# Reading V in its own layout in the first token mixes of a fused attention and mixer kernel, with V's copy, U's cast and the zero tile moved

One core of one Trainium2 chip. The metric is the device time of one execution in microseconds (us); lower is better. Most executions agree within 0.3%. Some executions fall in a slower state, with a lower clock; every ratio below uses runs of the fast state alone, while the medians quoted are of all runs.

## The reference

Random-feature attention for 8 batches, 8 heads, 576 tokens and head size 64, then a mixer on its output:

```python
def phi(x):
    proj = np.einsum('bhsd,md->bhsm', x, omega)
    return np.concatenate([np.cos(proj), np.sin(proj)], axis=-1) / np.sqrt(m)
kv  = einsum('bhsm,bhsd->bhmd', phi(k), v);   z = sum(phi(k), axis=2)
x   = (phi(q) @ kv) / (phi(q) @ z)            # all heads side by side: (B, 576, 512)
u   = x + (x.T @ U @ V).T                     # token mix, rank 32
out = u + np.maximum(u @ w_ch1, 0) @ w_ch2    # channel mix, 512 -> 2048 -> 512
```

`U` is 576 x 32, `V` is 32 x 576. The change is in how `V` and `U` reach the token mix.

## The kernel before

The program builds a list of operations, each for one engine, and emits them in a stored order (`ORDER`) with stored buffers (`SLOTS`); engines are in-order. PE multiplies matrices; DVE (VectorE), ACT (ScalarE) and POOL (GpSimd) do the rest. Tokens are laid out as (p, j), token = 9 p + j, so a block of 64 tokens with one j has every ninth column of `V`. GpSimd (POOL) therefore makes a packed copy `Vb` after the load:

```python
NJ = 9
o_vl = pool_dma("Vl", ..., lambda _: nc.gpsimd.dma_start(V_f, moe_V.unsqueeze(0).to_broadcast([4, R, S])), ...)
def v_cast(_):
    vf = V_f.rearrange("q (p j) -> q j p", j=NJ)
    nc.gpsimd.tensor_copy(Vb[:, 0:8, :].rearrange("q (a x) p -> q a x p", a=2),
                          vf[:, 0:8, :].rearrange("q (x a) p -> q a x p", a=2))
    for n in range(2):
        nc.gpsimd.tensor_copy(Vb[:, 8 + n, :], vf[:, 8, :])
```

Batches 0 and 1 (`TMIX`) make the mixed u already transposed, on PE: four matmuls transpose x, one adds V times the low-rank product. The moving operand of that one is `Vb`. This happens four times a batch, and once a batch for the last 64 tokens in four small pairs:

```python
def up(_):
    for i in range(4):
        nc.tensor.matmul(ups.t[:, i*P:i*P+P], x.t[:, i, cs], ident, start=(i == 0), stop=False)
    nc.tensor.matmul(ups.t, hu.t[:, cs], Vb[:, 0:8, :], start=False, stop=True)      # 128x512
def upt(_):                                                                          # tails
    for ct in range(NCT):
        ...
        nc.tensor.matmul(o, hu.t[:, c], Vb[:, 8, :], start=False, stop=(ct == NCT - 1))   # 128x64
```

Later batches use `Vb` as stationary operand. Until 36 us of planned time the program pads PE with matmuls on a tile `zero`, meant to keep its clock up; `zero` is set with other small tiles (`fills`) on DVE. U's cast to bf16 runs on POOL.

## Time and profile before

| | before |
|---|---|
| time, median (range of the 3 runs known then) | 359.13 us (358.83 to 359.60) |
| span of the profiled run | 356.7 us |
| PE busy in 28.3 to 352.3 us | 323.7 of 324.0 us |
| first w1 matmul on PE | 32.4 us |

The span is the time from the first to the last instruction in the trace; the device time is some 2 us more. Until 28 us attention of the first batch runs at the pace of DVE and ACT (the front); from there PE has work without a break until the end (the body). Anything that adds PE work in the body adds to the time one to one. The 512-column matmul that the change touches has this row (columns: busy us, mean ns of one, idle us before):

```profile
L763 PE MATMUL pb<-Vb,hu 128*128 128x512 bf16 x8 | 3.0, 379 | 0.0
L774 PE MATMUL pb<-Vb,hu 128*128 128x64 bf16 x8 | 0.7, 192 | 0.0
```

379 ns is start to modelled end. What one costs PE in a stream is the distance to the next start; the chain shows it, for the same kernel (columns: start us, us, what):

```profile
29.97 0.22 PE pb L762 x4
30.20 0.22 PE pb L763
30.41 0.22 PE pb L762 x4
30.64 0.22 PE pb L763
```

So 0.22 us for the V matmul (L763), and as much for the four transposes of x (L762). Further words used below: an eviction is a copy out of PSUM, the memory in which matmul results land; a norm is DVE's division of one head pair's result by its sum, four to a batch, each started by a RECIPROCAL; a pair is two heads; w1 and w2 are the two products of the channel mix; hu is the low-rank product x.T @ U; the tails are the last 64 tokens.

### The profile page before, as it was taken

The page shows a single profiled execution, that of the slowest core. Times are in us where ns is not written, and L with a number is a line of the kernel's source. Part 1 is how long each engine was busy: PE and PEld are TensorE (multiplying, and loading weights), DVE is VectorE, ACT ScalarE, POOL GpSimd, SP SyncE. Part 2 cuts the span into 40 slices and gives each one's busy share as a digit, 9 for nine tenths or more (in the row PEclk, how much of TensorE's full clock was granted, in tenths as well). Part 3 has the DMA queues.
Part 4 walks back from the last instruction along what each step waited for, and adds up shares of the span by engine and source line. Part 5 has one row for each costly group of instructions (what it writes and reads, how often), then busy time and mean ns, then how long its engine had stood idle before and what let it go on. Part 6 is the DMA issues. An engine that isn't in the chain of part 4 may idle for free.

```text
span 356.7 us, 9538 instructions
## 1 busy us (share of the span) xinstructions
PE 343.7 (96%) x4102; PEld 188.7 (53%) x4102; DVE 256.8 (72%) x423; ACT 210.1 (59%) x270; POOL 83.1 (23%) x148
## 2 busy tenths in 40 slices
PE   5879999999999999999999999999999999999994
PEld 3666566555557554555545554565455544555541
DVE  5999998887876787898688887886887663342221
ACT  3998998678847675557573868673676621202000
POOL 8795617511022028115041110100000000000000
PEclk9989999999999999999999999999999999999999
DMA  8999999994458999588679623891041115004114
GB/s 142 173 183 206 181 197 173 187 117 69 91 88 123 196 162 180 109 113 153 100 123 161 109 39 71 131 176 21 15 102 34 32 44 118 2 2 112 37 31 118
DMA packets 67403, 39.45 MB, mean 111 GB/s; under 512 B 47264, under 2 KB 61600, under 8 KB 67360
## 3 DMA queue, kind: packets, MB, share of 16 engines
q0 software_dynamic: 17376, 18.36, 34.6%
q1 hardware_dynamic: 49904, 20.34, 32.3%
q8 instruction: 32, 0.52, 0.6%
q10 hardware_dynamic: 80, 0.13, 0.1%
q14 instruction: 11, 0.09, 0.1%
HBM read 37.11 MB, written 9.44 MB: 130 GB/s over the span
## 4 chain that ended last, share of the span: by engine, by line
PE 90%; DVE 6%; issue 1%; ACT 1%; DMA 1%; SPq 0%
PE pb L917 34%; PE pb L863 31%; PE pp L703 5%; PE pb L882 4%; PE pp L718 4%; PE pp L618 2%; DVE cc L680 2%; PE pp L830 2%; PE pb L632 1%; DVE tt L655 1%; PE pp L724 1%; DVE tt L666 1%; PE pb L594 1%; PE pb L789 1%; DMA om_f<-in_omega_dram 1%
## 5 line engine op out<-in xcount | busy, mean ns | idle before, releaser
L863 PE MATMUL pb<-uT,W1b 128*128 128x512 bf16 x512 | 122.6, 379 | 0.0
L917 PE MATMUL pb<-W2b,hid 128*128 128x512 bf16 x512 | 122.5, 379 | 0.0
L810 ACT ACTIVATE hid<-pb 128x512 bf16<-128x512 f32 x87 | 50.6, 596 | 58.3 <-PE pb L863 58.2
L687 ACT ACTIVATE f<-cc 128x1152 bf16<-128x1152 int16 (+1 forms) x64 | 73.4, 1160 | 12.9 <-DVE cc L680 11.8
L684 ACT ACTIVATE f<-tt 128x1152 bf16<-128x1152 int16 (+1 forms) x64 | 73.6, 1160 | 7.7 <-DVE tt L655 4.8
L917 PEld LDWEIGHTS <-hid 128*128 128x128 bf16 x512 | 48.1, 98 | 55.5 <-issue 2.9
L863 PEld LDWEIGHTS <-W1b 128*128 128x128 bf16 x512 | 47.6, 98 | 55.8 <-issue 3.5
L680 DVE TENSOR_SCALAR cc<-tt 128x1152 int32<-128x1152 int16 (+1 forms) x64 | 50.2, 790 | 0.9
L582 POOL COPY v<-vraw 128x576 bf16<-128x576 bf16 x32 | 21.7, 681 | 95.5 <-PE pp L625 69.9
L808 DVE TENSOR_SCALAR hid<-pb 128x512 bf16<-128x512 f32 x41 | 27.9, 687 | 17.8 <-PE pb L863 17.7
L655 DVE CAST tt<-pp 128x1024 int32<-128x1024 f32 x32 | 38.9, 1216 | 1.6 <-PE pp L618 1.5
L664 DVE CAST tt<-pb 128x512 int32<-128x512 f32 x48 | 32.4, 685 | 8.3 <-PE pb L632 8.3
L951 DVE TENSOR_TENSOR o<-pb,x 128x512 f32<-128x512 f32 x24 | 16.5, 689 | 25.5 <-PE pb L917 25.5
L733 DVE TENSOR_TENSOR x<-pp,rc 128x640 bf16<-128x640 f32 x32 | 26.4, 825 | 1.1
L703 PEld LDWEIGHTS <-f 64*128 64x128 bf16 x1152 | 20.0, 95 | 10.7 <-issue 5.8
L553 POOL DMA_DIRECT2D qk<-in_q_dram x32 | 17.9, 563 | 31.3 <-DMA qkt<-qk 27.4
L703 PE MATMUL pp<-v,f 64*128 64x65 bf16 x1152 | 23.6, 192 | 0.9 <-ACT qkt L804 0.7
L718 PEld LDWEIGHTS <-f 128*128 128x128 bf16 x512 | 20.6, 99 | 7.3 <-issue 1.7
L718 PE MATMUL pp<-kvb,f 128*128 128x65 bf16 x512 | 21.8, 195 | 1.5 <-DVE x L733 1.3
L553 POOL DMA_DIRECT2D qk<-in_k_dram x31 | 17.1, 555 | 22.0 <-DMA qkt<-qk 17.2
L835 DVE TENSOR_TENSOR x<-pp,x 128x1024 bf16<-128x1024 f32 (+1 forms) x18 | 18.6, 1043 | 4.8 <-PE pp L830 4.4
L581 POOL DMA_DIRECT2D vraw<-in_v_dram x32 | 18.8, 588 | 6.5 <-DMA W2b<-in_moe_w_ch_dram 3.8
(81 smaller groups left out, 296.3 us busy)
## 6 DMA issues: line engine op xcount, KB each, us to landing
out_dram<-o SPq DMA_DIRECT2D x71, 128.0 KB, 2.4
qk<-in_q_dram POOLq DMA_DIRECT2D x32, 144.0 KB, 5.1
vraw<-in_v_dram POOLq DMA_DIRECT2D x32, 144.0 KB, 6.0
qk<-in_k_dram POOLq DMA_DIRECT2D x31, 144.0 KB, 5.4
W1b<-in_moe_w_ch_dram POOLq DMA_DIRECT2D x2, 1024.0 KB, 11.2
W2b<-in_moe_w_ch_dram POOLq DMA_DIRECT2D x4, 512.0 KB, 13.8
uT<-x SPq DMA_TRANSPOSE x30, 2.5
qkt<-qk SPq DMA_TRANSPOSE x24, 4.8
```

Of the source, the lines that this page charges most:

```text
L553: nc.gpsimd.dma_start(qk.t[:, lo:lo + NJ, :], src[b, 2 * hp:2 * hp + 2].rearrange("h (p j) d -> (h p) j d", j=NJ))
L655: o_kc = add("kcp", "DVE", 1.14, rank, lambda _: nc.vector.tensor_copy(i32(tt.t)[:, 1280:2304], kps.t.rearrange("p a b -> p (a b)")), deps ...
L664: nc.vector.tensor_copy(i32(tt.t)[:, 640 * lo:640 * lo + 512], t.t)
L680: nc.vector.tensor_scalar(out=i32(cc.t)[:, 0:n], in0=tt.t[:, lo:lo + n, 0], scalar1=16384.0, scalar2=None, op0=ALU.add)
L684: nc.scalar.activation(out=fe.t[:, 1, lo:hi], in_=tt.t[:, lo:hi, 0], func=ACT.Sin, scale=SIN_SCALE)
L687: nc.scalar.activation(out=fe.t[:, 0, lo:hi], in_=cc.t[:, 0:n, 0], func=ACT.Sin, scale=SIN_SCALE)
L703: nc.tensor.matmul(kvp.t[:, hh, 65 * s:65 * s + 65], fe.t[pr, s, 1152 + P * jj:1280 + P * jj], v65.t[pr, KJ[jj], :], start=(jj == 0), stop ...
L718: nc.tensor.matmul(nps.t[:, hh, 65 * i:65 * i + 65], fe.t[:, s, c0:c0 + 128], kvb.t[:, hh, s, :], start=(s == 0), stop=(s == 1))
L808: nc.vector.tensor_scalar(out=o, in0=i, scalar1=0.0, scalar2=None, op0=ALU.max)
L810: nc.scalar.activation(out=o, in_=i, func=ACT.Relu)
L863: nc.tensor.matmul(hp_.t, w1h[:, ct, fs], uT.t[:, ct, 0:512], start=(ct == 0), stop=(ct == NCT - 1))
L917: nc.tensor.matmul(d, w, W2b[c4][:, f % 4, :], start=(f == 0), stop=(f == NFT - 1))
```

## The change

The intent: no wait of the first mixes for V's copy, POOL and DVE relieved in the front by moving that copy behind the first batches, U's cast off POOL, and PE padded from the first microsecond. The core of the diff; the lines of `ORDER` and `SLOTS` are replaced throughout and cut here, as are lines at the dots:

```diff
-        last = 0.3 + next(t + o.end - o.start for o, t in zip(order, at) if o.name == "fills")
+        last = 1.2
+    V_j = V_f.rearrange("q (p j) -> q j p", j=NJ)
     def fills(_):
-        nc.vector.memset(zero, 0.0)
-        nc.gpsimd.tensor_copy(Ub, U_f[:, 0:4, :])
...
-    o_uc = add("Uc", "POOL", 0.6, -4.7, u_cast, deps=o_ul + [o_z])
+        copy(_, Ub, U_f[:, 0:4, :])
...
+    o_uc = add("Uc", ("DVE", "ACT"), (0.35, 0.5), -1.62, u_cast, deps=o_ul + [o_z])
-    o_vc = add("Vc", "POOL", 1.0, -4.65, v_cast, deps=[o_vl])
+    o_vc = add("Vc", "POOL", 2.1, -0.5, v_cast, deps=[o_vl])
-            nc.tensor.matmul(ups.t, hu.t[:, cs], Vb[:, 0:8, :], start=False, stop=True)
-        o_u = add("u", "PE", 0.45, rank, up, deps=[o_hc, o_vc, o_id], uses=[ups, hu, x])
+            nc.tensor.matmul(ups.t.rearrange("q (a x p) -> q a x p", a=2, x=4), hu.t[:, cs], V_j[:, 0:8, :].rearrange(
+                "q (x a) p -> q a x p", a=2), start=False, stop=True)
+        o_u = add("u", "PE", 0.5, rank, up, deps=[o_hc, o_vl, o_id], uses=[ups, hu, x])
-                    nc.tensor.matmul(o, hu.t[:, c], Vb[:, 8, :], start=False, stop=(ct == NCT - 1))
+                    nc.tensor.matmul(o, hu.t[:, c], V_j[:, 8, :], start=False, stop=(ct == NCT - 1))
+        if b == 2:
+            o_vc.deps.append(ldq[6])
+        nc.vector.memset(zero, 0.0)          # ahead of the emitted list (comment added here)
```

The 64 elements of one j now lie 9 elements, 18 bytes, apart, and the matmul reads them so.

More of the change, by code (lines that the diff above doesn't have):

```diff
@@ L119 @@
 ORDER = """
-16 18 45 0 7 5 46 9 17a 21 23 10 73 19 6 74 22a 25 24a 12 8 49 102 28 27 101 47 50b 32 1 26 75 51 30 53 20 3 77
-170 52b 29 35 55 31 33 79 34 198 225 36 58 169 103 54 56 57 80b 37 78a 59 81 48 62 60 84 105 107 38b 83 61 2 253
-82 86 64 197 14 65 85 39 63 274 13 108b 76 273 66b 106a 226 91 109 87 89 40 67 112 110 4 11 90 88 92 113 68 93 104
-116 254 115 111 171 69 94b 41 15 117 114 95 70a 118 96 121 71 199 97 122a 119 120 123 98a 173 124 175 42b 43 44a
-72b 99 174b 125 177 1069 176b 100b 227 178 203 255 126a 127 172 334 201 181 335 180 134 204b 128b 184 231 202a 179
@@ L125 @@
-183 185 205 1071 232a 182 257 208 1070 135 200 136a 143 186 141 258b 259 142a 189 144a 206 260a 209 207 229 187
-210 190b 1072 137 188 230b 145 138a 235 211 213 131 132 275 191 212 146b 238 192 133a 129 130b 159 153 234 233
-160b 217 155 214 277 228 236 215 154a 218b 151 237 156b 261 216 149 239 264 152a 338 354 219 220 353 241 165 256
-163 150b 262 242 336 240 372 166a 245 243 355 373 263 193 164a 221 391 265 194a 267 276 357 222b 244 246b 161 266
-157 268 392 162b 167 269 168b 158a 247 248 147 376 139 270 460 337 148a 249 140a 479 278 250a 327 271 325 195 1079
@@ L130 @@
-272 324 374 326 251 279b 280 281 1080 1081 196b 328 282 1082 497 478 252b 329 331 223 393 283a 286 287a 498 224a
-1083b 330 284 333 1073 339 1074 356 332 285a 344 345 320 321a 346 312 300 302 351 340b 343 347 341 459 301a 461
-303a 308 1075 288 313b 309b 348 349 342 395 350 1076 1077a 358 363 375 364 289a 306 362 1091 352 365 359b 307a 360
-298 366 367 299a 361 292 368 310 480 394 499 293b 369 311a 371 370 1092 377 384 1093 1094 296 381 378b 1095b 1096
-383 382 386 385 379 318 380 314 1085 319b 387 297b 388 315a 396 397a 451 390 389 450 294 449 1086 316 295a 452 517
@@ L135 @@
-398 290 317a 454 463 453 1087 455 399 1088 516 400 291a 464 1089b 584 456 1109 457 401a 465a 468 462 1110 469 471
-1111 410 472 470 1112 1084 406 411 1113b 304 407 482 305a 603 1114 402 474 1097 412 1098 1099 458 473 1100 476 322
-403 483 323a 429 1101b 488 1103 1104 475 481 487 466 1078 430a 489 518 409 477 604 491 1105 500 501 490 484b 485
-493 467 486 1106 447 1107a 492 502 448b 1115 495 494 404 405 408 417 1102 418a 509 519 496 421 507 623 422a 642
-503a 585 506 510 1108 508 514 1116 520 588 709 431 512 511 586 433 1117 622 1118 1119a 1120 504 505 441 607 434a
@@ L140 @@
-437 442b 513 432a 521 445 438a 522b 605 515 577 574 425 446a 426a 419 575 578 439 420a 576 581 523 524 729 427
-440a 580 626 428b 641 579 413 435 436b 525 526a 747 414a 589 423 594 595 593 624 443 590a 767 1121 766 598 596
-1122 535 424a 643 444a 583 527 536 415 1123 582 528 587 1124 597 416b 600 1125b 601 531 602 591 606 599 645 1127
-1128 1129 1130 532 592 1131 608 612 613 616 1139 1090 537 710 615 529 1140 1141 625 1142 835 614 554 1143 609b 617
-530 534 619 533 568 748 728 569b 618 555b 627 631 562 563a 1132 711 570 1144 634 610 730 632 544 644 635 633 712
@@ L145 @@
-571a 558 620 628a 637 636 611 545a 546 547b 638 640 559b 853 1133 1134 646 702 556 1135 731 699 749 572 557b 621
-629 700 713 639 701 1136 630 548 560 647b 750 648 1137 732 1145 1146 707 573b 561a 704 703 705 649 1147 1148 768
-751 1149 714 872 549a 715b 720 650 836 719 873 1157 892 651b 721 550 706 718 722 552 959 1126 1150 540 770 551a
-553a 541a 660 661 662 564 834 565b 855 652 653 723 654 656 726 657 1158 708 542 543b 566 567a 716 658 655 538 979
-717 724 1159 539a 1160 1161 659 733 679 680a 1163 737 739 725 738 741 1164 1165 743 742 1166 673 689 740 854 874
@@ L150 @@
-674a 1167 1138 727 769 734a 978 1151 744 752 1152 758 690a 667 745 669 756 753a 759 746 670a 735 671 757 760 668b
-762 761 687 754 688a 891 672a 736 764 763 755 683 838 1153 1154 1155 893 684b 837 1168 771 857 825 824 827 765
-1169 772b 663 664a 1170 826 961 829 960 828 773 774 1171 1172 1173 677 830 775 776b 831 839 675 846 678a 676a 843
-844 832 685 840b 691 777 1174 693 845 692a 695 847 876 781 849 1175 782 694a 778 696a 833 856 784 686a 681 682a
-980 1176 848 841 785 1177 850 786 842 851 665 666b 1162 787 875 1178 1179 858 863 859b 1193 862 866 865 867 1194
@@ L155 @@
-1195 1196 783 864 868 1197 852 869 822 823a 780 877 883 1187 1188 871 878b 881 1189 860 998 870 999 894 884 804
-1156 882 1190 962 885 888 890 887 886 861 805b 889 779 796 816 797b 817b 1191 697 798 895 896 698b 950 799a 818
-952 963 788 897b 951 982 808 949 879 789a 880 819a 898 899 809a 1211 1212 1213 794 900 795a 800 901a 1180 802 801b
-906 954 953 803b 820 907 1198 812 997 1001 821a 902 955 903 1214 814 905 904 981 956 813a 1215 964 815a 958 790
-791a 965a 1199 971 792 968 957 1200 969 810 970 973 966 972 1201 1202 806 793b 967 974 811a 976 1203 975 977 909
@@ L160 @@
-983 984a 988 989 807a 987 991 1192 990 908 993 992 1181 1182 985 1183 1184 1185 941 942a 986 913 1205 994 995 1002
-914a 1206 1207 1208 1000 1006 1007 1010 996 1009 1008 1013 1003b 945 931 915 1004 1014 1204 1186 1209 1011 1012
-1005 1210 1217 1218 916a 1016 935 1015 1017a 1018 1219 932b 1220 1019 910 1020 1021a 936a 927 946a 921 1221 911
-1222 1229 937 1026 1030 922a 925 926a 1230 928a 938b 1031 1022 919 920a 1027 1023 1231 1232 1233 912 933 1032 939
-1028 917 918b 940b 1223 934a 1029 1224 1225 1025 943 944b 923 924a 1226 1024 1037 1057 1227 1247 1216 1033 1038b
@@ L165 @@
-1034a 1053 1248 1059 1054b 1058a 1060a 1047 1048b 1249 947 1035 1036b 948b 1043 1250 1251 1061 1062b 1234 929
-1044b 1253 1254 1255 1256 1257 930a 1051 1052a 1063 1064b 1049 1065 1235 1050a 1258 1066a 1236 1237 1238 1045 1239
-1046b 1228 1055 1041 1056a 1039 1241 1252 1042a 1067 1068b 1242 1243 1244 1245 1265 1266 1240 1040b 1267 1259 1260
-1261 1262 1268 1246 1271 1272 1273 1269 1277 1274 1275 1270 1278 1279 1280 1276 1283 1263 1264 1281 1282 1284 1285
-1286 1287 1288 1289
+18 6 16 45 5 46 0 74 8 73 19 7 17a 12 9 10 21 23 24b 22a 25 49 28 27 30 102 26 3 50b 29 47 32 101 51 75 170 52b 20
@@ new lines @@
+53 31 35 56 34 33 54 57 79 103 55 58 80b 36 59 77 78b 198 83 225 48 86 1 62 37 4 60 38b 169 197 81 253 82 84 107
+274 85 63 105 61 39 64 76 273 106b 88 2 11a 254 87 65 40 66b 90 109 112 108a 226 89 67 68 92 91 93 110 111 104 41
+113 14 116 94a 115 171 69 95 70b 114 71 117 42a 121 119 43 118 96 97 120 122a 123 15 199 44b 98b 72a 175 173 203
+172 176b 124 99 204a 201 178 227 181 334 255 335 1069 179 174b 100b 202b 125 126b 182 231 177 259 127 232b 1070
+180 260b 229 205 134 230a 183 208 128b 143 144b 184 145 207 200 1071 210 206 185 189 146a 135 257 187 190b 186
@@ new lines @@
+258b 209 131 141 233 136a 188 235 211 213 1072 228 137 132 236 138a 142b 238 129 191 256 153 192 275 155 133a 159
+277 263 215 214 160b 212 338 354 217 234 237 156a 154a 151 353 336 216 163 165 239 218b 240 152b 241 130a 243 147
+266 262 276 166b 242 261 264 245 164a 355 244 372 148a 265 267 193 194a 157 149 219 220 246b 373 247 161 150a 391
+158a 248 139 162b 268 167 249 269 140a 168b 250a 270 278 357 272 325 221 324 392 327 1079 271 1080 279a 1081 13
+222b 329 459 280 376 460 195 326 328 1082 330 1083b 331 478 281 497 223 196b 251 252b 1073 224a 282 283a 339 346
@@ new lines @@
+284 285a 344 345 333 340b 1074 1075 332 343 312 313b 337 292 347 308 293b 309a 341 302 350 395 479 320 374 342
+303b 298 349 348 299a 1076 351 321b 358 1077a 498 1091 364 393 365 296 461 359b 362 363 366 300 352 1092 297a 367
+463 301b 356 1084 360 361 368 286 287b 314 315b 516 375 1093 369 480 377 382 371 394 384 306 370 1094 378a 381 462
+307a 584 499 318 379 319a 518 383 1078 386 517 385 316 380 585 322 323b 288 317b 1095b 1085 387 289a 388 396 603
+389 290 390 449 1086 397b 452 586 398 481 450 454 294 1087 1088 451 291a 310 453 399 455 311a 295b 1089b 464 456
@@ new lines @@
+465a 469 400 401b 1109 1110 1090 406 468 482 458 457 1111 410 473 472 407 411 1112 1113b 412 474 470 1114 500 402
+466 623 403 467 304 471 476 1097 605 501 475 1098 1099 1100 483 305a 1101b 447 488 641 487 477 404 489 405 1103
+484b 1104 1105 1106 492 408 491 448a 493 490 502 506 519 507 409 1107b 624 429 642 1115 485 430a 495 508 709 494
+496 520 728 511 443 604 509 431 1102 486 1116 1117 503a 510 504 1118 439 513 444a 512 505 515 432a 417 1096 418a
+1119a 521 440b 577 575 427 428a 522b 413 1120 414a 574 578 425 423 576 421 422b 514 523 524 426a 580 424a 437 588
@@ new lines @@
+415 579 438a 441 747 442a 416b 622 589 581 595 593 525 526b 583 435 596 1121 607 582 445 1108 535 626 536 590b 645
+436b 587 606 433 446a 434b 748 594 597 601 643 419 537 420a 600 527 528 1122 710 1123 1124 1125b 598 591 531 1127
+592 599 1128 532 1129 1130 1131 608 625 612 572 609b 613 617 533 616 615 614 1139 1140 619 1141 1142 618 767 602
+573a 627 1143 1133 534 1132 1134 631 530 529 1144 834 633 713 621 711 620 632 635 1126 1135 634 610 766 628b 636
+637 611 638 1136 729 1137 554 555a 564 570 571a 640 552 553a 565b 646 550 560 702 639 699 644 540 732 853 629 712
@@ new lines @@
+561a 556 647a 700 551a 648 701 704 541a 630 1145 703 706 557a 649 1146 1147 1148 1149 705 730 714 720 650 651b 707
+718 1157 749 568 652 731 750 751 721 569a 719 722 1150 566 1158 653 562 872 656 657 567a 544 542 708 715b 545b 725
+563a 655 546 558 726 716 543b 547a 892 658 717 548 891 549b 1159 1160 1161 538 723 559a 724 733 737 659 539a 1163
+1164 654 1138 770 739 835 738 741 727 693 742 740 768 1165 694b 836 683 1166 734a 743 769 752 684b 753b 960 1167
+744 746 838 1151 756 689 854 735 690a 757 1152 855 758 665 660 761 666a 745 736 760 762 759 677 675 661 1153 676b
@@ new lines @@
+763 1154 1155 678a 1156 979 771 1169 772b 826 825 764 824 765 827 828 1170 874 691 754 1168 857 830 667 668a 773
+755 774 1171 837 692a 1172 1173 1162 831 685 829 839 846 686a 775 776b 1175 832 978 1176 843 687 844 848 777 845
+851 840a 873 847 778 1177 850 856 876 833 669 670a 695 781 785 786 782 663 696a 671 662 688a 664b 841 672b 959 681
+673 893 842 783 849 682a 674a 1178 1179 697 858 863 1193 1194 1195 1196 862 866 859a 787 864 865 869 698a 867 868
+1197 784 780 679 895 877 680a 881 875 822 1187 852 779 823a 882 883 1174 885 860 861 884 870 804 805b 1188 886
@@ new lines @@
+1189 888 878b 792 887 961 793b 871 896 897b 1190 951 806 889 950 890 879 1191 949 880 807a 1198 1211 898 952 1180
+820 821a 794 899 1212 953 795a 900 901a 788 955 798 906 956 907 997 954 1213 789a 902 903 894 814 963 998 799a
+1214 1192 904 1215 964 969 982 958 815a 970 968 808 1199 796 965a 1200 957 797a 971 1201 973 972 974 810 800 975
+1202 909 811a 802 966 1203 803b 962 977 1181 816 817a 801b 905 809b 967 1182 812 983 990 908 813a 1183 988 987 976
+818 1184 992 989 819b 790 991 939 940a 910 791a 1185 994 919 920a 915 923 993 1205 916a 984a 980 981 911 1001 1002
@@ new lines @@
+996 1186 1008 995 1216 1206 1006 1007 1207 1010 931 1208 999 924a 932b 985 1209 1012 933 1009 1217 1003a 1011 921
+1218 1004 1000 986 922b 1013 1210 1014 1005 937 1016 1219 938a 1220 1017b 912 934b 1221 1015 1204 917 941 918a
+1018 1229 1019 1230 1231 942a 1020 1021b 935 936a 1232 1022 945 1233 1026 925 926a 913 1223 914a 927 1234 1224
+1225 1023 1025 946b 1027 928a 1226 943 1030 1024 947 1227 1028 1031 1029 944a 1247 1248 1249 1063 948b 929 1250
+1064a 1051 1045 1251 1235 1252 930a 1046b 1033 1236 1034b 1041 1052a 1053 1054b 1039 1237 1032 1040b 1047 1238
@@ L170 @@
+1239 1240 1042a 1049 1055 1048b 1050a 1056b 1241 1242 1243 1057 1058a 1244 1245 1037 1035 1036b 1038b 1067 1253
+1254 1068b 1228 1061 1222 1059 1043 1255 1062a 1256 1044a 1265 1246 1065 1257 1060a 1258 1266 1267 1268 1269 1270
+1066a 1277 1259 1260 1278 1271 1272 1273 1274 1275 1276 1279 1280 1281 1261 1262 1283 1263 1282 1264 1284 1285
+1286 1287 1289 1288
 """
 SLOTS = """
-001010200003111100201004001150030221101100001102321011000012131000120101200110100120001121320301010102120010201300
-101210110011111120102022110001402003101115201001202001101003201112010112031101110302000010102020112011201101220111
@@ L174 @@
-020131001220010203010210012110112021012210141001021012025100001021002001020101000100201013311003101101002200001220
-101321101202110132002112200004103201150132003110010012112101200100011210003102201010131001212002110122020010211230
-110011310200110320121320010402200510012211010120211010100011200230200001010021100111102121001010121022100022101101
-320010210223010222201002132010211010120011000211300101111010010013011120200210021002002103110202102011000110121312
-10102100010102201101030200201111000110110112000012101012102101002102001102100110010011200002012211021
+001200100011130110024010010031221510110101100201230100121001103012001100011210110100000211213311001223010202001011
@@ new lines @@
+010120111201103211001002141012102000101025211100201000011010011021001011321022131100010100222111001210132201102110
+100102101200004302102100011531101101012021020011210200102001201001000211212301103002300110001201011101000130003204
+112120101021010321100221000021015103200110021031012211010202100100011031020001001011001112101200001120130121002211
+210000121121020010032023301230012112011421122101010022000110010021510100102011011020001020210300201112101110200110
+110020230201021100022100101101120020001100300011011211101200110020112020010210100010201120200111121220110213110201
@@ L179 @@
+10002000112002223011202131011002032002112101010110001120111001011010100210200010001000210121202101120
 """
@@ L497, in u_cast @@
     def u_cast(_):
-        nc.gpsimd.tensor_copy(Ub, U_f[:, 0:4, :])
-        nc.gpsimd.tensor_copy(Ut[0:64, 0, :], U_f[0:64, 4, :])
-        nc.gpsimd.tensor_copy(Ut[64:128, 1, :], U_f[64:128, 4, :])
-    o_uc = add("Uc", "POOL", 0.6, -4.7, u_cast, deps=o_ul + [o_z])
+        copy(_, Ub, U_f[:, 0:4, :])
+        copy(_, Ut[0:64, 0, :], U_f[0:64, 4, :])
+        copy(_, Ut[64:128, 1, :], U_f[64:128, 4, :])
+    o_uc = add("Uc", ("DVE", "ACT"), (0.35, 0.5), -1.62, u_cast, deps=o_ul + [o_z])
     def pool_dma(name, rank, emit, work, dur, uses=(), deps=()):
@@ L509, in v_cast @@
     def v_cast(_):
-        vf = V_f.rearrange("q (p j) -> q j p", j=NJ)
         nc.gpsimd.tensor_copy(Vb[:, 0:8, :].rearrange("q (a x) p -> q a x p", a=2),
-                              vf[:, 0:8, :].rearrange("q (x a) p -> q a x p", a=2))
+                              V_j[:, 0:8, :].rearrange("q (x a) p -> q a x p", a=2))
         for n in range(2):
-            nc.gpsimd.tensor_copy(Vb[:, 8 + n, :], vf[:, 8, :])
-    o_vc = add("Vc", "POOL", 1.0, -4.65, v_cast, deps=[o_vl])
+            nc.gpsimd.tensor_copy(Vb[:, 8 + n, :], V_j[:, 8, :])
+    o_vc = add("Vc", "POOL", 2.1, -0.5, v_cast, deps=[o_vl])
     o_w1 = {}
@@ L773, in upt @@
                     nc.tensor.matmul(o, x.t[:, 4, c], ident[:, rows], start=(ct == 0), stop=False)
-                    nc.tensor.matmul(o, hu.t[:, c], Vb[:, 8, :], start=False, stop=(ct == NCT - 1))
-            o_t = add("ut", "PE", 0.24, rank + 0.0001, upt, deps=st["hc"] + [o_vc, o_id], uses=[tails, hu, x])
+                    nc.tensor.matmul(o, hu.t[:, c], V_j[:, 8, :], start=False, stop=(ct == NCT - 1))
+            o_t = add("ut", "PE", 0.24, rank + 0.0001, upt, deps=st["hc"] + [o_vl, o_id], uses=[tails, hu, x])
             st["tail"] = [add("utev", ("DVE", "ACT"), (0.34, 0.28), rank + 0.0001, lambda e: copy(
```

## The prediction

> **What bounds the kernel now.** I read the table of windows first, then the order of time on DVE and POOL in the front, then the chain, then the groups of instructions.
>
> Four windows split the span where PE stops being idle and where it does its last matmul:
>
> ```profile
> core 0: us, PE busy (x) PEld busy (x) DVE busy (x) ACT busy (x) POOL busy (x), PEclk, DMA share, GB/s
> 0.00:28.30 28.30, 19.94 (x361) 14.67 (x362) 23.74 (x45) 21.84 (x25) 23.13 (x45) 0.94 1.05 168
> 28.30:66.00 37.70, 37.53 (x597) 22.98 (x598) 35.03 (x60) 34.06 (x51) 20.48 (x34) 1.00 1.23 190
> 66.00:352.30 286.30, 286.20 (x3156) 151.00 (x3148) 197.44 (x319) 154.22 (x197) 39.47 (x71) 1.00 0.58 95
> ```
>
> From 28.3 us to 352.3 us PE is never idle (323.7 of 324.0 us), and after 352.3 only one eviction and its store are left. Matmul ends are modelled, so I checked the pace: the chain has the last w2 stretch as 92 matmuls in 19.87 us, 216 ns each, and four-matmul pieces of 0.86 us all the way from 41 us on. So the kernel is a front of 28.3 us, a PE-bound body of fixed work, and a tail of 4.4 us. A change can only shorten the front, let PE do more real work inside it, or alter the PE work itself. Of the 19.94 us of PE in the front, 6.5 us are matmuls on the zero tile, that is, padding.
>
> What bounds the front is DVE, with ACT almost as full (21.8 us). DVE starts the angle casts at 6.28 us and then hardly pauses until 28.9 us:
>
> ```profile
> 17.58 0.41 DVE L802 COPY qkt<-pb 128x512 bf16<-128x512 bf16 x1
> 17.91 1.74 DVE L680 TENSOR_SCALAR cc<-tt 128x1152 int32<-128x1152 int16 x1
> 19.57 0.21 DVE L731 RECIPROCAL pp<-pp 128x10 f32<-128x10 f32 x1
> ...
> 29.51 0.23 DVE L731 RECIPROCAL pp<-pp 128x10 f32<-128x10 f32 x1 [0.57 <-PE pp L724]
> ```
>
> POOL in the same stretch, from its own order of time:
>
> ```profile
> 17.84 1.15 POOL L511 COPY Vb<-V_f 128x512 bf16<-128x512 bf16 x1
> 18.89 1.13 POOL L514 COPY Vb<-V_f 128x64 bf16<-128x64 bf16 x2
> ...
> 21.63 0.32 POOL L498 CAST Ub<-U_f 128x128 bf16<-128x128 f32 x1
> 21.87 0.23 POOL L499 CAST Ut<-U_f 64x32 bf16<-64x32 f32 x1
> 22.16 0.64 POOL L500 CAST Ut<-U_f 64x32 bf16<-64x32 f32 x1
> ```
>
> The reader is to see the first DVE line with a long time, 1.74 us at 17.91: the same add on the same 1152 columns takes 0.75 us in the median of its line (0.684/0.754/1.735 us over the 16 before 60 us). It starts 0.07 us after POOL begins V's permuting copy and ends as that is done. So V's copy costs DVE 1.0 us on the path that sets the front. U's cast on POOL beside the add at 21.89 (0.84 us) costs 0.09 us.
>
> **What the Trainium skill says.** "GPSIMD Engine Reference", section 8, Key points, says that GpSimd shares its SBUF interfaces with VectorE and contends with it in a 2-port mode or with two SBUF inputs. The trace agrees: the SBUF-to-SBUF add goes from 0.75 to 1.74 us, while casts out of PSUM keep 1.21 to 1.23 us beside POOL's copies. Its section 7 gives about 2.9 cycles an element for a read with a step over 8 bytes. V's step is 9 bf16 elements, 18 bytes; 512 elements at 1.2 GHz would be 1.24 us, an estimate from that page, and the copy shows 1.154 us.
>
> "SBUF — State Buffer", Door 1 (the note on cachelines), says that full bandwidth needs at least two hits per 16-byte line. The new moving operand steps 18 bytes, so every element is on another line. The page gives no size for the penalty on a matmul, and no matmul before reads so: with the packed copy the 512-column one is at 379 ns, and its 216 ns spacing is that of the w1 matmuls.
>
> "TensorE: Matmul & The Clock Gate", What's actually happening, says that PE starts at half clock and needs one busy window of some 3.4 us. The trace agrees: 128-column matmuls take 0.31 us at 4.1 us and 0.22 us from about 10.6 us; a second slow stretch (clock 0.62 on average) is at 20 to 24.5 us.
>
> **The change, part by part.**
>
> V's copy behind: DVE gets back 1.74 - 0.75 = 1.0 us. POOL gets back 1.15 + 1.13 = 2.3 us in a stage where its 23.1 us are mostly DMA issues. The copy now stands after the load of q for pair 12, which is issued at 55 to 57 us before; Vb is first needed by the batch-2 mix, 101 us before. There it may again stretch a DVE add by 1 us, but PE then has two batches of w1 and w2 queued.
>
> U's cast: POOL gives up 1.2 us, DVE gets three small casts. A 128x128 cast takes DVE 0.28 us and its two half tiles should be smaller: I estimate 0.4 us. So 0.09 + 1.0 - 0.4 = 0.7 us are left for DVE. The waits they replace were not binding: V landed at 12.7 us and was copied by 20.0, U was cast by 22.8, and the first hU ran at 24.9 behind other PE work with no wait for Ub or Vb shown.
>
> The new order: up to the fourth norm, DVE gives two 512-column q/k evictions and two hu casts to ACT and takes one q/k eviction, one kvb cast, one hu cast and one uT eviction. By start-to-start distances that is -0.66 - 0.45 + 0.41 + 0.42 + 0.25 + 0.60 = +0.6 us on DVE; ACT gets the rest, and it has about 2.7 us of pauses between 6.8 us and its last uT eviction at 32.5. Before, one of the uT evictions came just after the fourth norm anyway. The gain of 0.7 us is therefore spread over two full engines: I count 0.4 to 0.7 us of earlier w1. PE also has three to five more transposes and angle matmuls of the second batch ahead of the first w1 matmul, 0.2 to 0.3 us each; that fills holes rather than moves the end. Sum for the front: -0.7 us, uncertain by about as much.
>
> Zero tile first: zero is set at 4.65 us today, so no padding can run before. Now DVE can set it at about 0.8 us, and PE is fed from about 1 us. If that ends the half clock before 6 us, the first transposes and the kang group (1.14 and 0.56 us on the chain) shrink by up to 0.4 us. The gate may also just open later. The same step puts the memsets of uT (0.60 us on POOL) ahead of the second k load, whose landing at 6.12 us releases PE's transposes at 6.17, ahead of qang: up to 0.3 us lost on DVE. I let these cancel, at -0.1 us.
>
> V as strided operand: eight 512-column matmuls and eight 64-column ones. If each element costs two cycles, a large one goes from 216 to about 430 ns. The two large ones of batch 0 that still run in the front are hidden; six of 0.21 us and the small ones (8 x 0.03) lie in the PE-bound body: +1.5 us. If the array hides it, 0. The planner's entry for this group grew only from 0.45 to 0.5 us, which I read as the author's expectation, not as a time; I weigh 0 to 0.3 us at 60% and 1.5 us at 40%, and enter +0.6 us in the middle.
>
> Sum: -0.7 - 0.1 + 0.6 = -0.2 us; the most likely single branch, a cheap stride, gives about -0.7. I put 358.7 us, from 359.13.
>
> **Rivals.** (1) The stride is dear. For: the cacheline rule, 18 bytes against 16. Against: the planner's entry. Result: the front gain is eaten, 359.5 to 360.3 us. (2) The first w1 load becomes the bound. It was issued at 16.6 us and landed at 27.7; the first w1 matmul ran at 32.4. It now stands behind four more q/k loads that land some 0.7 us apart: landing near 30.5 us, before the need. A 2 us slip more would cost PE 1 us: 360 us. (3) The front gains more than DVE's balance says, because POOL, free of 3.5 us, issues loads earlier and both engines lose their pauses: w1 starts 1.5 to 2 us earlier, 357.3 us. Against: DVE had only 0.57 us of idle time before the fourth norm, and DMA share is already over 1.0.
>
> **Range and chances.** Every part is under 2 us of 359, and 91% of the span is a PE body that the change does not touch, so 2% (7.2 us) is out of reach unless the new order stalls badly. 8 in 10: 357.4 to 360.1 us.
>
> **What would show it.** Right: no 1.7 us add in the front, zero matmuls from about 1 us, PE without idle time from about 27.5 us, a chain of PE alone after it. The stride is read from the spacing of the u matmuls: about 0.22 or 0.43 us. Wrong: PE waits on the W1 transfer around 32 us, DVE idle between 6 and 28 us, or PE idle at 50 to 66 us where V's copy now lies.

## The result and the profile after

The changed kernel took 365.02 us (364.46 to 365.47, 4 runs) beside 359.37 us for before (4 runs, one more than above). The ratio is 1.0157, 95% interval 1.0136 to 1.0178. Ratios here and below are the mean time of one kernel's fast runs over that of the other's of the same rounds, so not quite the ratio of the medians quoted. The time grew by about 5.6 us, and lies 5 us above the upper end of the predicted range.

The two V matmuls in the changed kernel, from the instructions that read `V_f` (min/median/max ns, first and last start in us):

```profile
L762 PE MATMUL pb<-V_f,hu x8: 1081/1082/1085, 25.8 to 72.3; 128*128 128x512 bf16 x8
L774 PE MATMUL pb<-V_f,hu x8: 276/276/282, 42.8 to 87.7; 128*128 128x64 bf16 x8
```

1082 ns against 379, with hardly any spread (the second row is the 64-column one: 276 against 192). And the chain of the changed kernel, where L761 are the transposes and L762 is the V matmul:

```profile
65.43 0.22 PE pb L761 x4
65.65 0.92 PE pb L762
66.57 0.86 PE pb L917 x4
67.44 0.22 PE pb L761 x4
67.66 0.92 PE pb L762
68.58 0.23 PE pb L761 x4
68.80 0.92 PE pb L762
```

The V matmul holds PE 0.92 us where it held 0.22: 0.70 us more, eight times, 5.6 us. The 64-column one takes 0.12 us in the chain (0.03 before): eight times 0.09, 0.7 us. Sum: 6.3 us of PE time. Two of the eight large ones start at 25.8 and 27.8 us, where PE had been padding before; the rest are in the body.

The stretches of the changed kernel show where PE is slowed or idle:

```profile
core 0: us, PE busy (x) PEld busy (x) DVE busy (x) ACT busy (x) POOL busy (x), PEclk, DMA share, GB/s
0.00:28.30 28.30, 21.09 (x383) 15.48 (x384) 22.83 (x46) 22.18 (x27) 20.01 (x38) 1.00 1.03 161
28.30:36.00 7.70, 7.52 (x96) 4.27 (x96) 5.93 (x12) 5.89 (x12) 3.56 (x7) 1.00 1.14 209
56.00:76.00 20.00, 18.05 (x228) 9.20 (x229) 13.77 (x25) 10.90 (x14) 12.43 (x21) 1.00 1.12 136
```

The reader should not be misled by "PE busy": between 28.3 and 36 us PE counts as busy for 7.52 of 7.70 us, yet two slow V matmuls are in it, and the first w1 matmul runs at 35.7 us instead of 32.4. (Not all of that is the operand's: in e9 below, the same kernel with step 1, it runs at 34.1: 1.7 of the 3.3 us come with the rest of the change.) A slow operand read is busy time, not a wait; no list of waits shows it. The 1.95 us without work between 56 and 76 us are nearly one gap:

```profile
59.04 0.22 PE L617 MATMUL pp<-WT,qkt 64*128 64x128 bf16 x1
61.05 0.39 PE L617 MATMUL pp<-WT,qkt 64*128 64x128 bf16 x7 [1.79 <-issue]
```

"issue" means that no semaphore was waited for. It was not there in the second profile of the same kernel (e11 below), whose span is 363.2 us against 363.7. That alone does not acquit the gap, as in e11 the first w1 matmul ran 1.5 us later (37.2 us, after a granted clock of 0.64 at 24.5 to 28.3 us). But e1 below has the loss without any gap: PE is busy 30.00 of 30.00 us at 36 to 66 us. So the gap is not needed for the loss; what held the instructions up, and what it cost this one profile, is open.

What the change was for did happen. DVE's add, 1.74 us beside V's copy before, is back to its usual time, but U's casts now stand ahead of it:

```profile
17.60 0.37 DVE L802 CAST Ub<-U_f 128x128 bf16<-128x128 f32 x1
17.73 0.91 DVE L802 CAST Ut<-U_f 64x32 bf16<-64x32 f32 x2
18.66 0.76 DVE L679 TENSOR_SCALAR cc<-tt 128x1152 int32<-128x1152 int16 x1
```

### The profile page after: what moved, and what is told of

Its sections match the earlier page's. It is cut to its first block, busy times and chain, and to the rows that moved or that the text cites. A ratio compares the mean times of both kernels' runs of the same rounds, so it can differ in the third digit from the quotient of the medians.

```text
span 363.7 us, 9535 instructions
## 1 busy us (share of the span) xinstructions
PE 346.2 (95%) x4065; PEld 190.2 (52%) x4121; DVE 253.8 (70%) x419; ACT 214.4 (59%) x277; POOL 83.6 (23%) x145
## 3 DMA queue, kind: packets, MB, share of 16 engines
q0 software_dynamic: 17376, 18.36, 35.7%
## 4 chain that ended last, share of the span: by engine, by line
PE 90%; DVE 5%; issue 2%; DMA 1%; ACT 0%; DVEq 0%; ACTq 0%; POOLq 0%
PE pb L917 34%; PE pb L863 30%; PE pp L702 5%; PE pb L882 4%; PE pp L717 4%; PE pb L762 2%; PE pp L617 2%; PE pp L830 2%; PE pb L631 1%; DVE tt L654 1%; DVE cc L679 1%; DMA qk<-in_q_dram 1%; PE pp L723 1%; PE pb L789 1%; PE pb L593 1%
## 5 line engine op out<-in xcount | busy, mean ns | idle before, releaser
L917 PE MATMUL pb<-W2b,hid 128*128 128x512 bf16 x480 | 118.9, 379 | 2.1 <-issue 0.6
L810 ACT ACTIVATE hid<-pb 128x512 bf16<-128x512 f32 x83 | 48.4, 596 | 62.0 <-PE pb L863 61.9
L863 PEld LDWEIGHTS <-W1b 128*128 128x128 bf16 x512 | 47.9, 98 | 56.2 <-issue 2.9
L581 POOL COPY v<-vraw 128x576 bf16<-128x576 bf16 x32 | 22.5, 706 | 103.2 <-PE pp L624 51.1
L808 DVE TENSOR_SCALAR hid<-pb 128x512 bf16<-128x512 f32 x45 | 30.3, 685 | 9.0 <-PE pb L863 8.8
L552 POOL DMA_DIRECT2D qk<-in_k_dram x31 | 18.4, 596 | 40.9 <-DMA qkt<-qk 39.1
L702 PE MATMUL pp<-v,f 64*128 64x65 bf16 x1152 | 23.2, 190 | 1.0 <-ACT f L686 0.7
L882 PEld LDWEIGHTS <-W1b 128*128 128x128 bf16 x512 | 16.7, 98 | 3.4 <-issue 1.1
```

The costliest lines, as they stand in the source:

```text
L552: nc.gpsimd.dma_start(qk.t[:, lo:lo + NJ, :], src[b, 2 * hp:2 * hp + 2].rearrange("h (p j) d -> (h p) j d", j=NJ))
L702: nc.tensor.matmul(kvp.t[:, hh, 65 * s:65 * s + 65], fe.t[pr, s, 1152 + P * jj:1280 + P * jj], v65.t[pr, KJ[jj], :], start=(jj == 0), stop ...
L810: nc.scalar.activation(out=o, in_=i, func=ACT.Relu)
L863: nc.tensor.matmul(hp_.t, w1h[:, ct, fs], uT.t[:, ct, 0:512], start=(ct == 0), stop=(ct == NCT - 1))
L882: nc.tensor.matmul(htp.t[:, 64 * k_:64 * k_ + 64], W1b[f // 8][:, ct, k_ * P:k_ * P + P], uT.t[:, ct, 512 + 64 * bpar:576 + 64 * bpar], st ...
L917: nc.tensor.matmul(d, w, W2b[c4][:, f % 4, :], start=(f == 0), stop=(f == NFT - 1))
```

## The experiments

Theory: the 18-byte step alone slows the matmuls and makes the loss. Rivals: the new order and later loads; the 1.79 us gap (in my expectations a "fetch stall", a name that no run supports). Jobs ran on different chips, so each kernel is compared with before on its own chip.

**e1: before, with only the operand changed.**

```diff
-            nc.tensor.matmul(ups.t, hu.t[:, cs], Vb[:, 0:8, :], start=False, stop=True)
+            nc.tensor.matmul(ups.t.rearrange("q (a x p) -> q a x p", a=2, x=4), hu.t[:, cs],
+                             V_j[:, 0:8, :].rearrange("q (x a) p -> q a x p", a=2), start=False, stop=True)
```
(and the same in the tails)

> The kernel before with only the operand of the u and ut matmuls changed to V's own layout; V's copy, U's cast, zero and the order stay. Theory (the 18-byte step makes a 512-column matmul cost 0.92 us instead of 0.22, and a 64-column one 0.12 instead of 0.03): six to eight of them on the path, 4.8 to 6.3 us more, 364 to 365.7 us. Rival (the new order and later loads cost the time): 359.0 to 360 us.

Measured: 365.48 us beside 359.79 (4 and 7 runs, one of the 4 slow), ratio 1.0122 (1.0057 to 1.0187), on a noisy chip. The profiled span is 362.4 us, 5.7 more than before's, with before's order, loads and copy:

```profile
L764 PE MATMUL pb<-V_f,hu x8: 1081/1082/1084, 27.8 to 69.3; 128*128 128x512 bf16 x8
```

The operand alone makes the loss, as far as this interval can tell; the next run closes in from the other side.

**e9: the changed kernel with step 1.**

```diff
-            nc.tensor.matmul(ups.t.rearrange(...), hu.t[:, cs], V_j[:, 0:8, :].rearrange(...), ...)
+            nc.tensor.matmul(ups.t, hu.t[:, cs], V_f[:, 0:512], start=False, stop=True)
-                    nc.tensor.matmul(o, hu.t[:, c], V_j[:, 8, :], ...)
+                    nc.tensor.matmul(o, hu.t[:, c], V_f[:, 512:576], ...)
```

> The changed kernel, letter for letter, but the u and ut matmuls read the first 512 and the last 64 columns of V as they lie, with step 1: the result is wrong on purpose, every instruction, wait and load stays. If the step alone costs the time: the matmuls at 0.38 us again, 8 x 0.70 + 8 x 0.09 = 6.3 us less PE work, 358.5 to 359.5 us. If order, loads or a fetch stall take part: 360.5 us or more.

Measured: result wrong; 360.63 us beside 359.5 (6 and 11 runs), ratio 1.0026 (0.9990 to 1.0061).

```profile
L762 PE MATMUL pb<-V_f,hu x8: 379/379/391, 25.8 to 67.2; 128*128 128x512 bf16 x8
```

The same instructions in the same order with the same waits, and the loss is gone but for a rest that is not clear of zero. The profiled span is 357.5 us. The median lies above my band and just inside the rival's (360.5 or more). Before's own 359.5 on that chip explains little of it; one of the six runs was slow, and the fast ones scatter from 359.27 to 362.69. So most of the 1.57% is the step; by the interval up to 0.6%, some 2 us, may by this run alone belong to order, loads or the gap. e7 and e12 below keep the new order and loads with a packed copy, and narrow that to 0.1 and 0.2% at most.

**e2 and e5: the rest of the change, and the new order alone, with packed V.** e2 is the changed kernel with `Vb` as operand again and the copy on POOL moved ahead; e5 is before with nothing but the new order and slots.

```diff
 e2 (from the changed kernel):
-            nc.tensor.matmul(ups.t.rearrange(...), hu.t[:, cs], V_j[:, 0:8, :].rearrange(...), ...)
+            nc.tensor.matmul(ups.t, hu.t[:, cs], Vb[:, 0:8, :], start=False, stop=True)
 ... (the same in the tails; both wait for V's copy again, which no longer waits for the load of q)
 ORDER: 13 (V's copy) moved ahead of the third v copy on POOL
 e5 (from before): ORDER and SLOTS of e2, nothing else
```

> The changed kernel with the packed copy of V as operand and the copy on GpSimd moved early, just ahead of the third v copy; order, U's cast and zero as changed. Theory (stride): the loss is gone, 358 to 360 us. Rival (order, loads, an instruction-fetch stall near 60 us): still 363 us or more.

> The kernel before with nothing but the new order and buffer slots; V packed and copied early, U cast on GpSimd, zero set with the other fills. Stride theory: 358.5 to 360 us, within 0.3% of before. Rival (order is at fault): 362 us or more.

Measured, both in the noisy job: e2 360.62 us, ratio 1.0009 (0.9957 to 1.0061); e5 360.25 us, 0.9981 (0.9926 to 1.0036), beside 359.79. Both medians lie just above my bands, and far under the rivals'. The order does not make the loss. But the second rival of the prediction, the late w1 load, does show once V's copy and U's cast are on POOL under the new order. POOL issues the first w1 load at 23.76 us in e5 (21.76 in the changed kernel), and PE waits for it:

```profile
34.85 1.47 PE L861 MATMUL pb<-uT,W1b 128*128 128x512 bf16 x6 [1.70 <-DMA W1b<-in_moe_w_ch_dram]
```

In e2, where only V's copy is on POOL, the load lands at 34.91 us and the first w1 matmul follows at 34.95. In the changed kernel it lands at 30.05 us, and that wait is absent. So in these profiles moving V's copy behind is what keeps this order of loads from binding.

**e3: before, with only the zero tile first.**

```diff
-        last = 0.3 + next(t + o.end - o.start for o, t in zip(order, at) if o.name == "fills")
+        last = 1.2
     def fills(_):
-        nc.vector.memset(zero, 0.0)
     with tc.manual_schedule():
+        nc.vector.memset(zero, 0.0)
```

> The kernel before with only the zero tile set first and padding from about 1 us. If an earlier warm-up shortens the front: 0.2 to 0.5 us faster. If DVE bounds the front whatever PE's clock: 359.0 to 359.5 us, no change.

Measured: 360.40 us beside 359.79, ratio 1.0006 (0.9945 to 1.0068): nothing resolved. The ratio fits "no change", the median lies above that band. Padding runs from 0.99 us, but the first transposes and angle matmuls at 4 to 7 us keep their slow durations, and DVE's first cast starts at 6.65 us (6.28 before). That start scatters anyway: it is at 7.01 us in e1, whose front begins as before's does.

**e4: before, with only U's cast on DVE.**

```diff
-        nc.gpsimd.tensor_copy(Ub, U_f[:, 0:4, :])   (and the two Ut)
+        copy(_, Ub, U_f[:, 0:4, :])                 (and the two Ut)
-    o_uc = add("Uc", "POOL", 0.6, ...)
+    o_uc = add("Uc", ("DVE", "ACT"), (0.35, 0.5), ...)
 ORDER: 11 (U's cast), and the loads of U before it, ahead of the third pair's key add
```

> The kernel before with only U's cast moved to DVE, just ahead of the third pair's key add. If DVE bounds the fourth norm: its three casts (about 1 us in the changed kernel, against my estimate of 0.4) add 0.3 to 0.9 us, 359.5 to 360.3. If the fourth norm waits for ScalarE and PE anyway: 359.0 to 359.6.

A first build of it was refused by the memory check, as the cast came ahead of U's loads in the program; the loads were moved too. Measured: 361.6 us beside 359.92 (6 and 11 runs), ratio 1.0040 (1.0010 to 1.0070), slower by more than I expected:

```profile
18.16 1.19 DVE L800 CAST Ub<-U_f 128x128 bf16<-128x128 f32 x1
19.27 1.11 DVE L800 CAST Ut<-U_f 64x32 bf16<-64x32 f32 x2
20.41 0.76 DVE L678 TENSOR_SCALAR cc<-tt 128x1152 int32<-128x1152 int16 x1
```

The add is fast, but now the casts stretch beside POOL's copies, to 2.25 us start to start. Counted from DVE's first cast (6.77 us here), the first norm begins 1.0 us later than before, the fourth 2.0 us later. The second microsecond came after the casts: PE ran short of work (busy 1.69 of 4.50 us at 20 to 24.5 us), and its granted clock was 0.50 at 24.5 to 28.3 us and 0.83 at 28.3 to 36; which of the two led to the other was not tested. Taken alone, with U's loads later too, this part costs.

**e8: before, with only V's copy on ACT and DVE.**

```diff
-        nc.gpsimd.tensor_copy(Vb[:, 0:8, :].rearrange(...), vf[:, 0:8, :].rearrange(...))
-        for n in range(2):
-            nc.gpsimd.tensor_copy(Vb[:, 8 + n, :], vf[:, 8, :])
+        nc.scalar.copy(Vb[:, 0:8, :].rearrange(...), V_f.rearrange(...)[:, 0:8, :].rearrange(...))
+    def v_last(_):
+        nc.vector.tensor_copy(Vb[:, 8:10, :], V_f.rearrange(...)[:, 8:9, :].to_broadcast([P, 2, D]))
 ORDER: the first where ACT waited, ahead of the third pair's last cosine; the second ahead of the fourth norm
```

> The kernel before with only V's copy moved from GpSimd to ScalarE (ahead of the third pair's last cosine, where ScalarE waited 0.71 us) and the last block to DVE. If the contention of GpSimd's copy with DVE's add cost the front 1 us: the add at 18 us is 0.75 us again, the fourth norm 0.5 to 1 us earlier, 358.2 to 359 us. If the front is bound elsewhere: 359.0 to 359.6.

Measured: 359.35 us beside 359.5 (6 and 11 runs), ratio 0.9995 (0.9967 to 1.0023). DVE's order of time in e8:

```profile
18.69 0.80 DVE L679 TENSOR_SCALAR cc<-tt 128x1152 int32<-128x1152 int16 x1
...
30.11 0.23 DVE L730 RECIPROCAL pp<-pp 128x10 f32<-128x10 f32 x1 [0.95 <-PE pp L723]
```

The add is at 0.80 us, and counted from DVE's first cast (6.98 us in e8, 6.28 before) the first norm begins 12.4 us after it instead of 13.3. But the fourth begins 23.1 us after it instead of 23.2: DVE waits 0.95 us for PE, which waits for ACT's last functions of the fourth pair, and ACT had to make the copy. ACT's order of time, before and in e8:

```profile
22.76 1.16 ACT L687 ACTIVATE f<-cc 128x1152 bf16<-128x1152 int16 x1 [0.71 <-DVE cc L680]
...
22.51 1.14 ACT L508 COPY Vb<-V_f 128x512 bf16<-128x512 bf16 x1
23.53 1.19 ACT L686 ACTIVATE f<-cc 128x1152 bf16<-128x1152 int16 x1
```

Before, ACT waited 0.71 us for DVE's add and began this function 16.5 us after DVE's first cast. In e8 it was free after 15.5 us, one microsecond earlier, and spent that on the copy: 1.14 us, where it evicts 512 contiguous columns in 0.59. So DVE's microsecond is real and did reach ACT; e8 moved the cost of the copy from DVE to ACT, and does not show that it was worth nothing. No run takes the copy away and changes nothing else. In e5, where the add takes 0.80 us, the fourth norm begins 22.1 us after the first cast, but e5 has the new order too, and then waits for the w1 load.

**e7 and e12: the changed kernel with that same copy.**

```diff
 V's copy as in e8, from the changed kernel; the u matmuls read Vb, step 1
 ORDER: the first ahead of the fourth pair's key sine on ACT, the second ahead of the fourth norm on DVE
```

> The changed kernel with a packed copy of V again, but made by ScalarE in its 0.85 us pause ahead of the fourth pair's sine (one instruction, about 0.6 us) and, for the last block, by DVE in its 0.54 us pause ahead of the fourth norm. Stride theory: as fast as with step 1, 358.3 to 359.5 us, and correct; POOL stays free, so W1 lands near 30 us as in the changed kernel.

> The changed kernel with V's packed copy on ScalarE and DVE once more, beside the change on one chip: stride theory says 5 to 6 us less than the change. Against before: 358.5 to 359.5 us; it beats before only if the interval lies under 1.

Measured, correct: e7 358.93 us beside 359.5, ratio 0.9980 (0.9951 to 1.0008); e12 359.79 beside 359.92, ratio 0.9991 (0.9959 to 1.0023), its median a little above my band. Its profiled run was a slow one and isn't read. The loss of the change is mended, but the interval does not lie under 1: no version here is shown to beat before.

**e11: the changed kernel once more.**

> The changed kernel itself, for a comparison on one chip with the two below: 364 to 366 us, 1.2 to 1.7% over before.

Measured: 364.67 us beside 359.92 on the chip of e12, ratio 1.0140 (1.0101 to 1.0178). e12 is 1.5% below it on the same chip, 0.9991 against 1.0140.

**e10: permute on the way out instead of on the way in.**

```diff
-            nc.tensor.matmul(ups.t.rearrange("q (a x p) -> q a x p", ...), hu.t[:, cs], V_j[...], ...)
+            nc.tensor.matmul(ups.t.rearrange("q (a x p) -> q p x a", a=2, x=4), hu.t[:, cs],
+                             V_f.rearrange("q (p j) -> q p j", j=NJ)[:, :, 0:8].rearrange("q p (x a) -> q p x a", a=2), ...)
```

> The changed kernel, but the large u matmul reads V almost as it lies (8 of 9 elements, step 1) and the permutation is in the order in which PSUM is written. If only the read of SBUF is bound by its lines: 0.22 to 0.25 us a matmul, 359 to 360 us, correct, with no copy before batch 2. If PSUM writes out of order are as slow: 0.9 us or more a matmul, 364 us or more.

Measured, correct: 361.33 us beside 359.92, ratio 1.0034 (1.0005 to 1.0064). One of the matmuls and the next PE instruction:

```profile
68.28 0.61 PE L762 MATMUL pb<-V_f,hu 128*128 128x512 bf16 x1
68.70 1.49 PE L918 MATMUL pb<-W2b,hid 128*128 128x512 bf16 x6
```

Start to start 0.42 us: neither of the two expected figures. This form costs 0.2 us a matmul more than the packed one, not 0.7. It has the scattered write and also a read that skips every ninth column; the two were not separated. It cuts the loss to 0.34%, from 1.40% for the change on that chip (e11), without any early copy. The tails, which still read with step 9 (276 ns each), are part of the rest.

**e6: a ladder of steps.** At the end of before, 16 matmuls for each step, same weights, same PSUM bank:

```diff
+        flat, bank = W1b[0].rearrange("q t f -> q (t f)"), ps.t[5]
+        for step in (1, 2, 3, 4, 5, 6, 7, 8):
+            for _ in range(16):
+                nc.tensor.matmul(bank, ident, flat[:, 0:512*step].rearrange("q (n s) -> q s n", s=step)[:, 0, :],
+                                 start=True, stop=True)
```

> The kernel before with 8 x 16 matmuls of 512 columns at its end, each 16 reading the w1 weights with a step of 1, 2, ... 8 elements. If two hits to a 16-byte line suffice: 0.22 us apart up to step 4 and rising from 5 to 8. If any step but 1 loses packed reads: a jump at step 2. The 18-byte step of V was at 0.90 us.

Eight stretches, each from the first start of one step to that of the next, of these instructions alone (us, PE and its weight loads busy, granted clock, DMA):

```profile
354.35:357.81 3.46, 3.46 (x17) 1.57 (x17) 1.00 0.28 76
357.81:361.42 3.61, 3.61 (x17) 1.53 (x16) 1.00 0.00 0
361.42:366.85 5.43, 5.43 (x17) 1.62 (x16) 1.00 0.00 0
366.85:374.07 7.22, 7.22 (x18) 1.84 (x17) 1.00 0.01 2
374.07:383.08 9.01, 9.01 (x17) 1.86 (x16) 1.00 0.00 0
383.08:393.90 10.82, 10.82 (x18) 1.98 (x16) 0.56 0.00 0
393.90:406.49 12.59, 12.59 (x18) 1.97 (x17) 0.50 0.00 0
406.49:421.07 14.58, 14.57 (x17) 1.86 (x15) 0.50 0.00 0
```

Divided by 16, a matmul takes 0.216, 0.226, 0.339, 0.451, 0.563, 0.676 and 0.787 us for steps 1 to 7. The last stretch includes the end of its last matmul; from its first start, 406.49, to its last, 420.0, lie 15 matmuls: step 8 takes 0.90. Both expectations fail. There is no plateau up to step 4 and no jump at 2: from step 2 on the time is the step times 0.113 us, in proportion to the bytes spanned. If 16-byte lines are what is counted (the Trainium skill gives this size in "SBUF — State Buffer", Door 1, the note on cachelines), step 2 spans 128 lines, step 4 256 and step 8 512, each at about 1.76 ns; an estimate from these figures. At step 1 the 64 lines would take 0.11 us, and the columns' own pace, 0.216, is the longer. Step 9 takes 0.90 us in the changed kernel from one start to the next (65.49 to 66.39 us; 0.92 in its chain), as much as step 8 and less than 9 x 0.113 = 1.02: in step with no more than one line an element. The clock fell to half at steps 6 to 8, and the proportion holds: the read, not the array, sets the pace there.

## Why the prediction was wrong

**What bounds the kernel** was right: a front, a body of PE alone, a short tail. It is why 0.7 us a matmul goes almost wholly into the time.

**The stride is the step that failed**, as a size: the term "V as strided operand". I allowed two cycles a column at the worst (0.43 us, +1.5 us in all), gave the hidden case 60% because the planner's entry had hardly grown, and entered +0.6 us. Measured were 0.92 us a matmul, four times the packed one, and 6.3 us of PE work in place of 0.6. Of this, 5.7 us show in the spans of e1 over before; that the rest lies in the slack of the front, where one or two of the large ones run, is argued and not shown. The mechanism (every element on a new line) was in the prediction; the skill gave no size, and a planner's constant was no substitute for one. With a slope unknown by a factor, the upper end of 360.1 us was too low: even two cycles a column left little room under it, and four had not been priced at all. The range was argued from a body "that the change does not touch", though the same prediction put six of the V matmuls into it.

**The front gain of 0.7 us** was not found: e9, which has all of the change but the step, is at +0.26% (-0.10 to +0.61). Two terms of it failed. U's cast cost DVE 1.06 us (17.60 to 18.66), not 0.4; its two last casts ran beside another POOL copy, and this alone takes up what the add gave back. And the prediction counted +0.6 us for the new order on DVE and then left it out of its sum for the front. In e9, counted from DVE's first cast, the first norm begins 0.44 us earlier than before and the fourth 0.11 us later: 0.55 us are lost between them.

**V's copy beside DVE's add**: the size was right. 1.74 us before, 0.76 in the change, 0.80 in e8. The reading that the add "ends as that is done" was not: POOL's large copy ends at 18.99 us, its small ones at 20.03, the add at 19.65. The add ends 0.65 us after the large copy, about the least time of its line (0.684), as if it had waited for that copy to end. The cast of `Ub` in e4 (18.16 to 19.35 us) ends 0.1 us after the same copy there. Such a wait is a reading of these times; no run was made to test it.

**Zero first**: about nothing, as entered (e3), within a wide interval. The -0.1 us was two guesses of 0.4 and 0.3 us set against each other. The first, an earlier end of the half clock, did not come: the matmuls at 4 to 7 us stayed slow. That the sum was right is luck.

**Rival 1, a dear stride**, was the right one, and its own figure of 359.5 to 360.3 too small. **Rival 2, the w1 load**: it landed at 30.05 us, near the 30.5 foreseen, and did not bind in the change; it does in e5. **Rival 3**, a freer front, did not come about.

**What stays open**: the 1.79 us gap in one profile, what DVE's microsecond would be worth if no engine had to take the copy, and effects under some 0.4%, which the runs of e7, e8 and e9 cannot tell from none.

## What to carry to other kernels

The layout of a matmul's moving operand is part of its price: in e6, for 512 columns of bf16, a step of 2 elements was all but free, 4 cost twice, and 8, like 9 in the change, four times, and the profile shows it only as longer PE busy time with no wait. Before taking a copy away, multiply that price by the number of matmuls that read the copy (here 8 x 0.70 = 5.6 us against a copy of 2.3 us on POOL, which held DVE up by 1.0 us), and where the size is unknown let the range cover it. A copy that disturbs another engine can be real contention, and moving it can still gain nothing, if the engine that takes it over is the next to be waited for, as ACT was in e8.

## What the Trainium skill lacked or had wrong

- "SBUF — State Buffer", Door 1 (the note on cachelines) says that bf16 can step 8 elements for free, and that two hits to a 16-byte line suffice. For a matmul's moving operand the runs differ: 0.226 us at step 2 (four elements a line), 0.451 at step 4 (two), 0.90 at step 8, against 0.216 packed (e6).
- No page prices a strided moving operand: "TensorE: Matmul & The Clock Gate" has columns and clock alone. Measured: the step times 0.113 us for 512 columns, from step 2 to 8, the same at a granted clock of 0.50.
- "PSUM — Partial Sum Buffer", Specifications, says that any non-contiguous access slows matmuls significantly, with no size. In e10 a matmul with a scattered write takes 0.42 us for 512 columns instead of 0.22; its read skips every ninth column, and what that adds was not separated.
- No page gives ScalarE's price for a step of 18 bytes: 1.14 us for 512 columns in e8. 512 contiguous ones take 0.59, but out of PSUM, so the source differs too.
